# Loads of the first block, the order of the first loads, and matmuls on ones at the head of an attention and MLP kernel

## Chip and metric

The kernel runs on one NeuronCore of a Trainium2 chip. The metric is the device time of one execution in microseconds; lower is better. Before the change it was 308.45 us, the median of three runs (308.12 to 308.74).

## What is computed

Sliding-window attention with a linear bias (ALiBi), and behind it a two-layer MLP with a squared ReLU. Cut to what matters:

```python
# q, k, v: (8, 8, 576, 64) float32;  w_in: (512, 2048);  w_out: (2048, 512)
rel = pos[:, None] - pos[None, :]
bias = slopes[:, None, None] * (-abs(rel))
mask = (rel >= 0) & (rel < 128)
attn = softmax(where(mask, q @ k.T / 8 + bias, -1e9))
x = (attn @ v).transpose(0, 2, 1, 3).reshape(4608, 512)
out = square(maximum(x @ w_in, 0)) @ w_out          # (4608, 512) float32
```

## The kernel before

**Tiles.** Each of the 8 sequences of 576 tokens is cut into five blocks of 128, 128, 128, 128 and 64 tokens; a block holds all 8 heads, so its k, q and v are 128 x 512 each. There are 40 blocks, and 9 groups of 512 tokens for the MLP. Because the window is 128, a block of queries needs its own keys and those of the block before it.

**Work of a block** (`attention(m)`): k and q are turned on TensorE by eight transposes into one PSUM tile (`tp`, L331) and copied to `kqT` in two halves (L304 on VectorE, L306 on ScalarE). The scores are 8 or 16 matmuls (`ps_s`, L361), ScalarE takes the exponential (`P`, L374), VectorE multiplies by a mask that holds both bias and window (L382), TensorE multiplies with v (`pv`, L397, where a column of ones in `vt` gives the row sum), VectorE divides (L418, L423) into `x`, and four transposes (`xp`, L442) with a copy (L304) put the block into `xT`. From block 10 the first transposes, and from block 13 the last, are done by the DMA queue of SyncE (SP) instead.

**Work of a group**: 16 columns of `w_in` chunks give `h` (L477), ScalarE takes the ReLU (`rt`, L487), VectorE or ScalarE squares it (`g`, L495, L497), and `w_out` is applied: plainly in group 0 (L628), in the others by a Strassen-like scheme of seven products (L559) on sums of blocks. Groups 0 and 1 take `h` block by block (`SPLIT`), since their tokens arrive one block at a time.

**Loads.** All loads are issued by GpSimd (POOL), which casts fp32 to bf16 on the way: k, q, v of a block (L290, 128 KB each in bf16), `w_in` in four quarters of columns (L256) and `w_out` in four quarters of rows (L263), 512 KB each. `FIRST` (L162) gives the order of the first ones: `b0` is block 0, `i0` the first quarter of `w_in`, `o0` that of `w_out`. Eight loads can be under way: the ninth waits for the first to land. k and q have four buffers in a ring, v has six.

**Order.** Nothing is ordered by hand. Every piece of work is a `Task` with the engines that can do it, a duration, a key, and the tasks and buffers that it needs. `Plan.order()` (L57) plays the tasks through once, always taking the one that can start earliest, lowest key first, and each engine's queue then holds its tasks in the order of the planned starts. On the chip an engine works its queue in that order, and an instruction that waits holds up all behind it. The durations and delays are the plan's own; `COLD` (L42) is the planned time up to which a task of TensorE counts double (L113), and L115 to L117 say when a planned load lands:

```python
dur = t.engs[e] * (2 if e == "PE" and st < self.COLD else 1)
if t.dma is not None:
    at = max(st + dur + 900.0, self.dma_free)
    self.dma_free = at + t.dma
    t.end = self.dma_free + 900.0
```

**Head of the kernel.** GpSimd writes `dist` with an iota (L208); VectorE makes `ident`, which the transposes need, and `far` and `dist` out of it (L214, L220 to L223); ScalarE makes the eight `masks` (L234). VectorE also sets the ones in `vt` (L240, L242).

Of the kernel before, what the change touches and what calls it, by code (L numbers as in the profile page):

```python
# [8 lines left out]
FP32 = mybir.dt.float32  # L9
BF16 = mybir.dt.bfloat16  # L10
# [26 lines left out]
class Plan:  # L37
# [1 line left out]

    LAT = {"PE": 260.0, "ACT": 290.0, "DVE": 270.0, "POOL": 200.0, "SP": 2200.0}  # L40
    BEGIN = {"POOL": 1250.0}
    COLD = 15000.0  # L42

    def __init__(self, bufs):
        self.tasks = []
# [11 lines left out]
    def order(self):  # L57
        used = {tag: [] for tag in self.bufs}
        free = {}
        cand = {}  # L60
        left = {}
        for t in self.tasks:
            left[t] = len(t.deps)
            for d in t.deps:
                d.users.append(t)
            for e in t.engs:
                free.setdefault(e, self.BEGIN.get(e, 800.0))
                cand.setdefault(e, [])
        for t in self.tasks:
            if not left[t]:  # L70
                for e in t.engs:
                    cand[e].append(t)

        def avail(t):
            at = t.ready
            more = {}
            for s in t.acq:
                if s.idx is not None:
                    continue
                u = used[s.tag]  # L80
                n = self.bufs[s.tag]
                more[s.tag] = more.get(s.tag, 0) + 1
                i = len(u) + more[s.tag] - 1 - n
                if i >= 0:
                    old = u[i]
                    if old.left:
                        return None
                    at = max(at, old.freed)
            return at

        done = []
        n_all = len(self.tasks)
        while len(done) < n_all:
            best = None
            for e, c in cand.items():
                lo = None
                for t in c:
                    a = avail(t)
                    if a is None:
                        continue  # L100
                    st = max(a, free[e])
                    k = (st, t.key, t.seq)
                    if lo is None or k < lo[0]:
                        lo = (k, t)
                if lo is not None and (best is None or lo[0][0] < best[0]):
                    best = (lo[0][0], e, lo[1])
            if best is None:
                raise RuntimeError("plan is stuck: " + repr([
                    (e, t.key, [s.tag for s in t.acq if avail(t) is None]) for e, c in cand.items() for t in c
                    if e != "POOL"][:40]))  # L110
            st, e, t = best
            t.eng, t.start = e, st
            dur = t.engs[e] * (2 if e == "PE" and st < self.COLD else 1)  # L113
            if t.dma is not None:
                at = max(st + dur + 900.0, self.dma_free)  # L115
                self.dma_free = at + t.dma
                t.end = self.dma_free + 900.0  # L117
            else:
                t.end = st + dur + (self.LAT[e] if t.lat is None else t.lat)
            free[e] = st + dur  # L120
            for x in t.engs:
                cand[x].remove(t)
            for s in t.acq:
                if s.idx is not None:
                    continue
                s.idx = len(used[s.tag]) % self.bufs[s.tag]
                used[s.tag].append(s)
            for s in t.rel:
                s.left -= 1
                s.freed = max(s.freed, t.end)  # L130
            for u in t.users:
                left[u] -= 1
                u.ready = max(u.ready, st + dur if e == "PE" and "PE" in u.engs else t.end)
                if not left[u]:
                    for x in u.engs:
                        cand[x].append(u)
            done.append(t)
        done.sort(key=lambda t: (t.start, t.seq))
        return done
# [3 lines left out]
def kernel(  # L143
    ctx: ExitStack, tc: tile.TileContext, q, k, v, moe_w_in, moe_w_out, out
):
    nc = tc.nc

    B, H, S, D = q.shape
# [8 lines left out]
    C = d_model // 128  # L157
# [1 line left out]
    NG = NT // 512  # L159
    NBLK = B * NKB  # L160

    FIRST = "b0 i0 b1 i1 b2 i2 b3 i3 b4 b5 b6 o0 b7 o1 b8 o2 b9 o3"  # L162
    SPLIT = ([(0, 128), (128, 256), (256, 384), (384, 512)], [(0, 256), (256, 512)])

    KQ_DMA, X_DMA = 10, 13
# [2 lines left out]
    const = ctx.enter_context(tc.tile_pool(name="const", bufs=1))  # L168
    psum = ctx.enter_context(tc.tile_pool(name="psum", bufs=2, space=bass.MemoryType.PSUM))
    work = ctx.enter_context(tc.tile_pool(name="work", bufs=2))  # L170

    ident = const.tile([128, 128], BF16)
# [14 lines left out]
    kq = ring("kq", size["kq"], [128, 2, d_model])  # L187
# [14 lines left out]
    def mm(n):  # L202
        return max(n, 64) / 2.4 + 1.5
# [4 lines left out]
        nc.gpsimd.iota(dist, pattern=[[-128, 2], [1, 128]], base=128, channel_multiplier=-1,  # L208
                       allow_small_or_imprecise_dtypes=True)

    t_iota = plan.add({"POOL": 360.0}, -9e5 + 0.012, build_iota)

    def build_ident():
        nc.vector.tensor_single_scalar(ident, dist[:, 1], 0.0, op=ALU.is_equal)  # L214
# [8 lines left out]
        nc.vector.tensor_tensor(dist, dist, far, op=ALU.add)  # L223

    t_dist = plan.add({"DVE": 1300.0}, -9e5 + 0.5, build_dist, [t_ident])
    t_mask = []

    def place(h):
# [50 lines left out]
    def load_block(m, key):  # L279
        b, kb = divmod(m, NKB)  # L280
        n = blk[kb]
        s_in[m, "k"] = s_in[m, "q"] = Slot("kq")
        s_in[m, "v"] = Slot("v")
        for i, (nm, src) in enumerate((("k", k), ("q", q), ("v", v))):
            sl = s_in[m, nm]

            def emit(i=i, src=src, sl=sl, nm=nm):
                o = (vt[sl.idx][0:n, :, 0:D] if nm == "v"
                     else kq[sl.idx][0:n, i].rearrange("s (h d) -> s h d", h=H))
                nc.gpsimd.dma_start(o, src[b, :, kb * 128:kb * 128 + n, :].rearrange("h s d -> s h d"))  # L290
            t_in[m, nm] = load(key + 0.01 * i, 1050.0 * n / 128, emit, [t_ones] if nm == "v" else [], [sl])
# [10 lines left out]
    def copy(task, o, i):  # L302
        if task.eng == "DVE":
            nc.vector.tensor_copy(o, i)  # L304
        else:
            nc.scalar.activation(o, i, AF.Copy)  # L306

    def attention(m):
# [10 lines left out]
        if kq_by_dma:  # L319
            def turn_kq():  # L320
                nc.sync.dma_start_transpose(kqT[sk.idx], kq[s_in[m, "k"].idx].rearrange("s t f -> s (t f)"))
            t_kq = [plan.add({"SP": 2000.0}, due - 80, turn_kq, [t_in[m, "k"], t_in[m, "q"]], [sk],
                             [s_in[m, "k"]], dma=1400.0)]
        else:
            slot = Slot("h" if first else "a")
            last = None
            for i in range(2 * C):
                def emit(i=i):
                    if i == 0:
                        slot.tile = psum.tile([128, 1024], BF16, tag=slot.tag, bufs=plan.bufs[slot.tag], name="tp")  # L330
                    nc.tensor.transpose(slot.tile[:, i * 128:(i + 1) * 128],  # L331
                                        kq[s_in[m, "k"].idx][:, i // C, (i % C) * 128:(i % C + 1) * 128], ident)
                last = plan.add({"PE": mm(128)}, due - 56, emit,
                                [last, t_ident, t_in[m, "kq"[i // C]]] + ([t_in[m, "q"]] + chain["tp"] if i == 0 else []),
                                [slot, sk] if i == 0 else [], [s_in[m, "k"]] if i == 2 * C - 1 else [])
            chain["tp"] = [last]
            t_kq = []
            for i in range(2):
                def evac(i=i):
                    copy(t_kq[i], kqT[sk.idx][:, i * C:(i + 1) * C, 0:n],  # L340
                         slot.tile[:, i * 512:(i + 1) * 512].rearrange("p (c s) -> p c s", c=C)[:, :, 0:n])
                t_kq.append(plan.add(both if first else {("DVE", "ACT")[i]: both[("DVE", "ACT")[i]]},
                                     due - 56, evac, [last], [], [slot]))
        t_kq_of[m] = t_kq


# [41 lines left out]
        for hf in range(2):  # L388
            slot_v = Slot("o" if m < 5 else "h")
            last = None  # L390
            for hi in range(4):
                h = 4 * hf + hi
                for part, mk in parts:
                    def emit(h=h, hi=hi, part=part, mk=mk, slot_v=slot_v):
                        if hi == 0 and part == p0:
                            slot_v.tile = psum.tile([128, 512], FP32, tag=slot_v.tag, bufs=plan.bufs[slot_v.tag], name="pv")
                        nc.tensor.matmul(  # L397
                            slot_v.tile[:, hi * (D + 1):(hi + 1) * (D + 1)],
                            Pt[sP.idx][:, place(h), part, :], vt[s_in[mk, "v"].idx][:, h, :],
                            start=part == p0, stop=part == 1)  # L400
# [242 lines left out]
    key = 0  # L643
# [15 lines left out]

    done = plan.order()  # L660
    kernel.plan = done
    with tc.manual_schedule():
        for t in done:
            t.emit()


# [28 lines left out]
```

## Time and profile before

| | us |
|---|---|
| median of three runs | 308.45 |
| the profiled execution | 308.27 |
| its span, first to last instruction | 306.1 |
| TensorE busy | 289.8 |
| VectorE busy | 212.2 |
| ScalarE busy | 200.0 |
| GpSimd busy | 107.6 |

The profile is of one execution. Times in its rows are counted in us from the first instruction. Engines are named PE (TensorE), PEld (its weight loads), DVE (VectorE), ACT (ScalarE), POOL (GpSimd) and SP (SyncE). A row of the timeline has start, length, engine, line, operation, output and inputs, how many instructions are merged in it, and in brackets how long the engine had been idle and what ended that. A row of the loads has the size of one transfer and the us from its issue to its landing. A row of the waits has who waited for what, us in total, how often, and the longest.

### The profile page before, as it was taken

What the parts mean: (1) busy time and instruction counts of PE and PEld (TensorE: products, weight loads), DVE (VectorE), ACT (ScalarE), POOL (GpSimd) and SP (SyncE); (2) the same over time, 40 slices, a digit from 0 to 9 for tenths busy, and PEclk for the clock granted to TensorE, in tenths of its full rate; (3) what the DMA queues carried; (4) which work ended last, traced back from release to release, by engine and by line L of the source; (5) the groups of instructions that cost most, each with busy time, mean ns of one, the idle gap of its engine ahead of it and who ended that gap; (6) DMA issues with size and microseconds to landing.
All of it is one profiled execution on the core that took longest, in us unless ns stands there. A gap on an engine that the chain in (4) does not pass through costs nothing.

```text
span 306.1 us, 7855 instructions
## 1 busy us (share of the span) xinstructions
PE 289.8 (95%) x3076; PEld 205.9 (67%) x3076; DVE 212.2 (69%) x633; ACT 200.0 (65%) x395; POOL 107.6 (35%) x133
## 2 busy tenths in 40 slices
PE   1489999999999999999999999999999999999995
PEld 1279987686866677666666666666766676666783
DVE  4348888749968786678758776677677785545622
ACT  4178894759769666767767787777667785564410
POOL 8747938626265444226361327132200000000000
PEclk9999999999999999999999999999999999999999
DMA  8999999999999999999999999999884112201223
GB/s 60 179 175 166 151 189 173 130 184 139 151 151 144 164 157 169 155 154 182 165 153 166 156 139 149 130 165 146 139 55 120 30 42 62 69 0 36 69 72 103
DMA packets 170901, 39.31 MB, mean 128 GB/s; under 512 B 158064, under 2 KB 170352, under 8 KB 170864
## 3 DMA queue, kind: packets, MB, share of 16 engines
q0 software_dynamic: 116736, 18.36, 93.9%
q1 hardware_dynamic: 54128, 20.46, 41.3%
q8 instruction: 24, 0.39, 0.5%
q14 instruction: 13, 0.11, 0.1%
HBM read 36.70 MB, written 9.44 MB: 151 GB/s over the span
## 4 chain that ended last, share of the span: by engine, by line
PE 92%; DMA 3%; DVE 2%; POOL 2%; ACT 1%; issue 0%; POOLq 0%; DVEq 0%
PE h L477 42%; PE o L559 32%; PE ps_s L361 6%; PE pv L397 6%; PE o L628 4%; DMA kq<-in_q_dram 3%; PE tp L331 1%; POOL kq L290 1%; PE xp L442 1%; ACT kqT L306 1%; DVE w_mix L273 0%; DVE kqT L304 0%; POOL vt L290 0%; DVE osb L593 0%; POOL w_in_sb L256 0%
## 5 line engine op out<-in xcount | busy, mean ns | idle before, releaser
L477 PE MATMUL h<-xT,w_in_sb 128*128 128x512 bf16 (+2 forms) x832 | 150.8, 316 | 0.3 <-DVE x L423 0.3
L487 ACT ACTIVATE rt<-h 128x512 bf16<-128x512 f32 x144 | 86.0, 600 | 61.9 <-PE h L477 54.2
L477 PEld LDWEIGHTS <-w_in_sb 128*128 128x128 bf16 x832 | 71.0, 99 | 35.4 <-DVE x L423 0.8
L374 ACT ACTIVATE P<-ps_s 128x512 bf16<-128x512 f32 (+1 forms) x160 | 71.1, 520 | 9.7 <-PE ps_s L361 9.5
L495 DVE TENSOR_TENSOR g<-rt 128x512 bf16<-128x512 bf16 x91 | 38.3, 422 | 35.1 <-ACT rt L487 34.4
L382 DVE TENSOR_TENSOR P<-P,masks 128x512 bf16<-128x512 bf16 (+1 forms) x160 | 54.4, 364 | 8.0 <-ACT P L374 6.5
L559 PEld LDWEIGHTS <-g 128*128 128x128 bf16 x512 | 47.9, 98 | 15.1
L290 POOL DMA_DIRECT2D kq<-in_k_dram x40 | 34.2, 855 | 55.6 <-DMA kqT<-kq 48.4
L290 POOL DMA_DIRECT2D vt<-in_v_dram x40 | 34.1, 856 | 52.8 <-PE pv L397 46.6
L559 PEld LDWEIGHTS <-S 128*128 128x128 bf16 x384 | 35.8, 98 | 11.7 <-issue 0.7
L559 PE MATMUL o<-w_mix,S 128*128 128x256 bf16 x256 | 38.7, 273 | 0.0
L559 PE MATMUL o<-w_mix,g 128*128 128x256 bf16 x256 | 37.5, 273 | 0.0
L559 PE MATMUL o<-w_out_sb,g 128*128 128x256 bf16 x256 | 36.9, 273 | 0.0
L290 POOL DMA_DIRECT2D kq<-in_q_dram x40 | 34.3, 857 | 2.0 <-DMA kq<-in_k_dram 1.3
L497 ACT ACTIVATE g<-rt 128x512 bf16<-128x512 bf16 x53 | 33.5, 632 | 1.3
L423 DVE TENSOR_TENSOR x<-pv,rec 128x256 bf16<-128x256 f32 (+1 forms) x80 | 33.3, 417 | 1.1
L397 PEld LDWEIGHTS <-P 128*128 128x128 bf16 x576 | 27.3, 98 | 8.9 <-DVE P L382 1.2
L397 PE MATMUL pv<-vt,P 128*128 128x65 bf16 x576 | 31.5, 194 | 0.6 <-DVE P L382 0.6
L418 DVE RECIPROCAL rec<-pv 128x4 f32<-128x4 f32 (+1 forms) x80 | 14.2, 177 | 14.6 <-PE pv L397 14.2
L361 PEld LDWEIGHTS <-kqT 64*128 64x128 bf16 x576 | 15.7, 96 | 11.1 <-issue 8.9
L361 PE MATMUL ps_s<-kqT 64*128 64x128 bf16 (+1 forms) x320 | 20.1, 216 | 0.8 <-DVE kqT L304 0.8
L361 PE MATMUL ps_s<-kqT,kqT 64*128 64x128 bf16 (+1 forms) x256 | 17.0, 214 | 1.4 <-ACT kqT L306 1.4
(41 smaller groups left out, 190.6 us busy)
## 6 DMA issues: line engine op xcount, KB each, us to landing
out_dram<-osb SPq DMA_DIRECT2D x35, 256.0 KB, 4.3
kq<-in_k_dram POOLq DMA_DIRECT2D x32, 128.0 KB, 7.1
kq<-in_q_dram POOLq DMA_DIRECT2D x32, 128.0 KB, 7.4
vt<-in_v_dram POOLq DMA_DIRECT2D x32, 128.0 KB, 8.2
w_in_sb<-in_moe_w_in_dram POOLq DMA_DIRECT2D x4, 512.0 KB, 9.8
w_out_sb<-in_moe_w_out_dram POOLq DMA_DIRECT2D x4, 512.0 KB, 10.0
kq<-in_k_dram POOLq DMA_DIRECT2D x8, 64.0 KB, 9.2
kq<-in_q_dram POOLq DMA_DIRECT2D x8, 64.0 KB, 8.9
```

The source lines that it names most:

```text
L290: nc.gpsimd.dma_start(o, src[b, :, kb * 128:kb * 128 + n, :].rearrange("h s d -> s h d"))
L361: nc.tensor.matmul(slot_s[2 * (c // 2) + half].tile.rearrange("p (c t q) -> p c t q", c=2, t=2)[:, c % 2, part, 0:n], kqT[sk_of[mk].idx][r ...
L374: nc.scalar.activation(view(Pt[sP.idx][:, 2 * i:2 * i + 2]), view(slot_s[i].tile.rearrange("p (c t q) -> p c t q", c=2, t=2)), AF.Exp, bia ...
L382: nc.vector.tensor_tensor(pt, pt, view(masks[:, 2 * i:2 * i + 2]), op=ALU.mult)
L397: nc.tensor.matmul(slot_v.tile[:, hi * (D + 1):(hi + 1) * (D + 1)], Pt[sP.idx][:, place(h), part, :], vt[s_in[mk, "v"].idx][:, h, :], star ...
L418: nc.vector.reciprocal(srec.tile[0:n, :], pv[0:n, :, D])
L423: nc.vector.tensor_tensor(xt[sx.idx][0:n, hf * 256:(hf + 1) * 256].rearrange("p (h e) -> p h e", h=4), pv[0:n, :, 0:D], srec.tile[0:n, :]. ...
L477: nc.tensor.matmul(slot.tile[:, f * w:(f + 1) * w], w_in_sb[:, cc, (fc + f) * 128:(fc + f + 1) * 128], xT[:, cc, g * 512 + lo:g * 512 + hi ...
L487: nc.scalar.activation(srt.tile, slot.tile, AF.Relu, bias=0.0, scale=1.0)
L495: nc.vector.tensor_tensor(o, i, i, op=ALU.mult)
L497: nc.scalar.activation(o, i, AF.Square)
L559: nc.tensor.matmul(bank.tile[:, t * 256:(t + 1) * 256], left(g, what, j)[:, t * 128:(t + 1) * 128], right(by, j), start=opens and j == 0 a ...
```

## The change

- k and q of block 0 are loaded as fp32 into two buffers of the pool `osb`, by the queues of SP (k) and ACT (q), and cast to bf16 by two VectorE copies. v of block 0 stays with GpSimd.
- Among GpSimd's first loads block 1 stands ahead of the first quarter of `w_in`, block 2 ahead of the second, block 3 ahead of the third and fourth. The iota goes to the head of GpSimd's queue.
- k and q of a block are turned as two chains of four transposes, with the eviction of k as soon as its own four are planned to be done, still in one PSUM tile. Block 0's evictions are both VectorE's.
- VectorE writes a tile of ones. TensorE starts with seven matmuls of 512 columns on it, and as the program is put out, where TensorE's planned start of a task leaves a gap between 6 and 12.5 us of planned time, 128-column matmuls on ones are put in for about 70% of it. Their results are not used. In the built program these are 3, 2 and 16, ahead of block 0's transposes, block 0's scores and block 0's product with v.
- In the plan, the time up to which TensorE is slower becomes 9 us, and a task of 250 ns or more counts 1.4 times there; early loads start sooner, move 1.2 times longer and land later. So the order changes on all engines, throughout.

```diff
-    COLD = 15000.0
+    COLD = 9000.0
+    FILL = 12500.0
...
-            dur = t.engs[e] * (2 if e == "PE" and st < self.COLD else 1)
+            dur = t.engs[e] * (1 if e != "PE" or st > self.COLD else 2 if t.engs[e] < 250 else 1.4)
             if t.dma is not None:
-                at = max(st + dur + 900.0, self.dma_free)
-                self.dma_free = at + t.dma
-                t.end = self.dma_free + 900.0
+                early = st < self.COLD
+                at = max(st + dur + (700.0 if early else 900.0), self.dma_free)
+                self.dma_free = at + t.dma * (1.2 if early else 1.0)
+                t.end = self.dma_free + (1300.0 if early else 900.0)
...
-    FIRST = "b0 i0 b1 i1 b2 i2 b3 i3 b4 b5 b6 o0 b7 o1 b8 o2 b9 o3"
+    FIRST = "b0 b1 i0 b2 i1 b3 i2 i3 b4 b5 b6 o0 b7 o1 b8 o2 b9 o3"
...
-    t_iota = plan.add({"POOL": 360.0}, -9e5 + 0.012, build_iota)
+    t_iota = plan.add({"POOL": 360.0}, -9e5 - 1, build_iota)
...
+    ones_w = const.tile([128, 512], BF16)
+    slot_w = Slot("o")
+    scratch = {}
+
+    def build_warm():
+        nc.vector.memset(ones_w, 1.0)
+
+    def warm(n, w):
+        for _ in range(n):
+            nc.tensor.matmul(scratch["tile"][:, 512 - w:512], ones_w[:, 0:128], ones_w[:, 0:w], start=True, stop=True)
+
+    def first_warm():
+        scratch["tile"] = psum.tile([128, 512], FP32, tag="o", name="warm")
+        warm(7, 512)
+
+    t_warm = plan.add({"DVE": 300.0}, -9e5 - 2, build_warm)
+    plan.add({"PE": 2100.0}, -9e5, first_warm, [t_warm], [slot_w], [slot_w])
...
+            if m == 0 and nm != "v":
+                st = Slot("osb")
+
+                def raw(src=src, st=st, nm=nm):
+                    st.tile = work.tile([128, 512], FP32, tag="osb", bufs=plan.bufs["osb"], name="raw")
+                    (nc.sync if nm == "k" else nc.scalar).dma_start(
+                        st.tile.rearrange("s (h d) -> s h d", h=H), src[b, :, 0:n, :].rearrange("h s d -> s h d"))
+
+                def cast(i=i, st=st, sl=sl):
+                    nc.vector.tensor_copy(kq[sl.idx][:, i], st.tile)
+                t_raw = plan.add({"SP" if nm == "k" else "ACT": 450.0}, -2e6, raw, [], [st], dma=1050.0)
+                t_in[m, nm] = plan.add({"DVE": 470.0}, key + 0.01 * i, cast, [t_raw], [sl], [st])
+                continue
...
-            for i in range(2 * C):
...
+            for j, nm in enumerate("kq"):
+                last = None
+                for i in range(C):
...
+                        nc.tensor.transpose(slot.tile[:, (j * C + i) * 128:(j * C + i + 1) * 128],
+                                            kq[s_in[m, nm].idx][:, j, i * 128:(i + 1) * 128], ident)
...
+                chain["tp"] = [last]
+
+                def evac(j=j):
+                    copy(t_kq[j], kqT[sk.idx][:, j * C:(j + 1) * C, 0:n],
+                         slot.tile[:, j * 512:(j + 1) * 512].rearrange("p (c s) -> p c s", c=C)[:, :, 0:n])
+                t_kq.append(plan.add({"DVE": both["DVE"]} if m == 0 else both if first else
+                                     {("DVE", "ACT")[j]: both[("DVE", "ACT")[j]]}, due - 56, evac, [last], [], [slot]))
...
+    idle = 6000.0
     with tc.manual_schedule():
         for t in done:
+            if t.eng == "PE":
+                if idle < t.start < plan.FILL:
+                    warm(int(0.7 * (t.start - idle) / (107.0 if t.start < plan.COLD else 56.0)), 128)
+                idle = max(idle, t.start + t.engs["PE"] * (2 if t.start < plan.COLD else 1))
             t.emit()
```

More of the change, by code (lines that the diff above doesn't have):

```diff
@@ L325, in attention @@
             slot = Slot("h" if first else "a")
-            last = None
-            for i in range(2 * C):
[L328 to L335, printed above, removed]
@@ L336, in attention @@
-            chain["tp"] = [last]
-            t_kq = []
[L338 to L343, printed above, removed]
+            t_kq = []
@@ new lines, in attention, with emit @@
+            for j, nm in enumerate("kq"):
+                last = None
+                for i in range(C):
+                    def emit(i=i, j=j, nm=nm):
+                        if i == 0 and j == 0:
+                            slot.tile = psum.tile([128, 1024], BF16, tag=slot.tag, bufs=plan.bufs[slot.tag], name="tp")
+                        nc.tensor.transpose(slot.tile[:, (j * C + i) * 128:(j * C + i + 1) * 128],
+                                            kq[s_in[m, nm].idx][:, j, i * 128:(i + 1) * 128], ident)
+                    last = plan.add({"PE": mm(128)}, due - 56, emit,
+                                    [last, t_ident, t_in[m, nm]] + (chain["tp"] if i == 0 else []),
+                                    [slot, sk] if i == 0 and j == 0 else [], [s_in[m, nm]] if j == 1 and i == C - 1 else [])
+                chain["tp"] = [last]
[4 more added lines that the diff above has]
+                                     {("DVE", "ACT")[j]: both[("DVE", "ACT")[j]]}, due - 56, evac, [last], [], [slot]))
@@ L396, in emit @@
                             slot_v.tile = psum.tile([128, 512], FP32, tag=slot_v.tag, bufs=plan.bufs[slot_v.tag], name="pv")
+                            if slot_v.tag == "o":
+                                scratch["tile"] = slot_v.tile
                         nc.tensor.matmul(
```

## The prediction

> **What bounds the kernel now.** I read the page's head and chain first, then TensorE's waits, then TensorE's timeline to 31 us, then the loads' issues and landings.
>
> ```profile
> span 306.1 us, 7855 instructions
> PE 289.8 (95%) x3076; PEld 205.9 (67%) x3076; DVE 212.2 (69%) x633; ACT 200.0 (65%) x395; POOL 107.6 (35%) x133
> PEclk9999999999999999999999999999999999999999
> PE 92%; DMA 3%; DVE 2%; POOL 2%; ACT 1%; issue 0%; POOLq 0%; DVEq 0%
> ```
>
> TensorE is busy 289.8 of 306.1 us and is 92% of the chain that ends last. What is not TensorE lies at the start, as its waits say (total, times, longest):
>
> ```profile
> PE tp L331 <- DMA kq<-in_k_dram: 8.3, 2, 5.1
> PE ps_s L361 <- ACT kqT L306: 1.4, 2, 0.7
> PE o L559 <- DVE osb L593: 0.5, 1, 0.5
> PE h L477 <- DVE x L423: 0.3, 1, 0.3
> ```
>
> The two waits for k are blocks 0 and 1. The timeline (start, length, what, idle before) gives the places:
>
> ```profile
> 7.80 0.61 PE L361 MATMUL ps_s<-kqT 64*128 64x128 bf16 x8 [0.85 <-DVE kqT L304]
> 8.97 1.18 PE L397 MATMUL pv<-vt,P 128*128 128x65 bf16 x8 [0.56 <-DVE P L382]
> 13.38 0.61 PE L331 MATMUL tp<-ident,kq 128*128 128x128 bf16 x4 [3.23 <-DMA kq<-in_k_dram]
> 16.93 3.24 PE L477 MATMUL h<-xT,w_in_sb 128*128 128x128 bf16 x32
> 20.22 0.61 PE L331 MATMUL tp<-ident,kq 128*128 128x128 bf16 x8
> 20.67 0.59 PE L397 MATMUL pv<-vt,P 128*128 128x65 bf16 x9
> 21.98 0.23 PE L361 MATMUL ps_s<-kqT,kqT 64*128 64x128 bf16 x2 [0.71 <-ACT kqT L306]
> 22.76 1.28 PE L477 MATMUL h<-xT,w_in_sb 128*128 128x128 bf16 x20
> 30.32 0.61 PE L331 MATMUL tp<-ident,kq 128*128 128x128 bf16 x8
> ```
>
> So h begins at 16.93, and from about 20 us on TensorE hardly stops. The same h costs 3.24/32 = 0.101 us at first and 1.28/20 = 0.064 later with its tail (about 0.056 apart, from the eight transposes at 20.22: 0.61 less one of some 0.22 over seven). The PEclk row shows no step there, yet the pace nearly doubles: up to about 20 us TensorE runs at half pace. Time can be won only ahead of 22 us, and stays won only if nothing later waits. The loads (POOL's issue, then one load's size and us to landing):
>
> ```profile
> 1.25 1.02 POOL L290 DMA_DIRECT2D kq<-in_k_dram  x1 [0.80 <-POOLq L679]
> 2.26 0.89 POOL L290 DMA_DIRECT2D kq<-in_q_dram  x1
> 4.55 0.76 POOL L256 DMA_DIRECT2D w_in_sb<-in_moe_w_in_dram  x1
> 5.29 0.91 POOL L290 DMA_DIRECT2D kq<-in_k_dram  x1
> 7.89 0.80 POOL L256 DMA_DIRECT2D w_in_sb<-in_moe_w_in_dram  x1
> 17.86 0.75 POOL L256 DMA_DIRECT2D w_in_sb<-in_moe_w_in_dram  x1 [1.29 <-DMA w_in_sb<-in_moe_w_in_dram]
> 19.79 0.68 POOL L290 DMA_DIRECT2D kq<-in_q_dram  x1
> ```
>
> ```profile
> kq<-in_k_dram POOLq DMA_DIRECT2D x1, 128.0 KB, 3.8
> kq<-in_q_dram POOLq DMA_DIRECT2D x1, 128.0 KB, 4.0
> w_in_sb<-in_moe_w_in_dram POOLq DMA_DIRECT2D x1, 512.0 KB, 7.9
> kq<-in_k_dram POOLq DMA_DIRECT2D x1, 128.0 KB, 8.0
> w_in_sb<-in_moe_w_in_dram POOLq DMA_DIRECT2D x1, 512.0 KB, 9.7
> w_in_sb<-in_moe_w_in_dram POOLq DMA_DIRECT2D x1, 512.0 KB, 10.0
> kq<-in_q_dram POOLq DMA_DIRECT2D x1, 64.0 KB, 9.3
> ...
> GB/s 0 0 0 96 90 90 109 123 182 189 160 158 180 203 201 162 158 176 205 201 165 157 173 211 198 167 157 155 161 147 118 103 114 179 158 182 157 163 181 203
> ```
>
> Row by row, issue plus landing: k0 5.05, q0 6.26, first quarter of w_in (w0) 12.45, k1 13.29, w1 17.59, w3 27.86, q4 29.09. The last row is the DMA rate in slices of 1 us. Two paces follow. Settled: k1 comes 0.84 after w0, so a block's three loads take 2.5; from k1 to w1 there are q1, v1 and w1, so a w_in quarter takes 4.3 - 1.7 = 2.6 (check: w1 to w3 is two blocks and two quarters, 10.2; the rows say 10.27). Early: q0 comes 1.21 after k0, at 90 to 109 GB/s against 157 to 211 later.
>
> **The loads.** The change issues k0 and q0 as fp32 from SP and ACT at about 0.75 (their queues are empty there; ACT's table load and masks wait for nothing that this issue delays), and POOL's queue becomes iota, k1, q1, v0, v1, w0, block 2, w1, block 3, w2, w3. No row shows an fp32 load of 256-byte pieces on these queues. The nearest are the last stores:
>
> ```profile
> out_dram<-osb SPq DMA_DIRECT2D x3, 256.0 KB, 2.2
> out_dram<-osb SPq DMA_DIRECT2D x2, 128.0 KB, 1.7
> ```
>
> By bytes, 256 KB lands 2.2 after issue, at 3.0. By pieces, the second 128 rows cost 0.5, and 1024 pieces would take 1.7 + 7 x 0.5 = 5.2, landing at 6.0. I take 4.5, the middle; POOL's own k0 took 3.8 with its 1.02 of issue. Five more 128 KB loads (the other raw one, k1, q1, v0, v1) at the early pace: 4.5 + 5 x 1.21 = 10.55. Then w0: 2.6 at the settled pace, or 5.0 as before (12.45 - 6.26 less one 1.21 for v0). It now moves when the rate row is already at 160 and more: 3.3, so w0 lands at 13.9. Ends: 3.0 + 5 x 0.84 + 2.6 = 9.8, and 6.0 + 6.05 + 5.0 = 17.0. Each later load follows at the settled pace: w1 at 13.9 + 2.5 + 2.6 = 19.0 (1.4 later than before, since block 2 goes ahead of it), q3 20.7, w3 26.7, q4 27.9 (q4 was 1.23 behind w3).
>
> [...]
>
> **Head of the kernel.** The casts are two DVE copies of 128x512. The nearest rows:
>
> ```profile
> 7.00 0.76 DVE L304 COPY kqT<-tp 128x512 bf16<-128x512 bf16 x2 [1.68 <-PE tp L331]
> 21.33 0.60 ACT L306 ACTIVATE kqT<-tp 128x512 bf16<-128x512 bf16 x1 [0.52 <-DVE kqT L304]
> 8.62 1.12 DVE L382 TENSOR_TENSOR P<-P,masks 128x256 bf16<-128x256 bf16 x4 [0.87 <-ACT P L374]
> ```
>
> 0.38 to 0.42 each, up to 0.6 for fp32; DVE idled 1.68 there, which covers them. On DVE the four kqT copies of blocks 0 and 1 now stand ahead of block 0's mask products, so these wait for q1 (4.5 + 3 x 1.21 = 8.1): block 0's pv begins near 9.8 instead of 8.97. That costs nothing, since block 1's ps_s, which waited until 15.97, can follow at about 10.5, and its exponentials and most of its pv lie in the wait for w0. If that cover went, the price would be the 0.8 of that delay.
>
> **Matmuls on ones.** Seven of 512 columns at half pace are 4 x 0.101 x 7 = 2.8 us, three of 128 another 0.3: from about 1.4 to 4.6, ahead of the first cast. Two and sixteen more stand ahead of block 0's ps_s and pv: 1.8 us at half pace, 1.0 at full, while DVE copies and multiplies. Cost nothing; without that cover 1.8, still ahead of w0. What they buy is the pace. The half pace cost 32 x (0.101 - 0.056) = 1.4 us before; now h is cut by waits until 22 us, so I book the pace within the next count and not again.
>
> [...]
>
> **Count at 22.8 us.** Before, 32 h are done there, and block 2's pv, block 3's transposes and ps_s are not. After, from 13.9 on, TensorE does 16 h each of blocks 0 and 1 on w0, all of attention 2 but pv's end, then at 19.0 twelve h on w1, block 3's transposes at 20.7, eleven h, block 3's ps_s near 22: 55 h. Ahead: 23 x 0.056 = 1.3, pv 0.5 (nine take 0.59 at 20.67; its last few are still to come), xp 4 x 0.056, transposes 8 x 0.056, ps_s 0.45 (eight took 0.61 at half pace, sixteen are needed): 2.9 us. The loads cap it: q4 at 27.9 is 1.2 earlier, and before, TensorE took q4 1.2 after it landed (30.32 against 29.09), so at most 2.4 is kept.
>
> **Split transposes.** In blocks 0 to 9 k's four transposes are now evicted ahead of q's four. Both share one PSUM tile, and in the built program q's transposes wait for the eviction of k in blocks 0 to 5, 8 and 9; before, none did. Behind such a transpose everything on TensorE queues. One costs the eviction (0.42 on DVE, 0.60 on ACT) less what stands between: in blocks 2 and 3 it hides behind q's landing, 0.84 after k's; in 4, 5, 8, 9 five h or a few transposes (0.28) stand there, leaving 0.1 to 0.3. Ends: nothing, or the 0.71 that ps_s waited for the same copies at 21.98. I take 0.7 in all. The rest of the order is replanned; I book nothing, as the waits after 22 us were single and 1.5 in total.
>
> Sum: 2.4 - 0.7 = 1.7 us. The profiled execution took 308.27 (span 306.1 and 2.2 around it), 0.2 under the median 308.45: 308.3 - 1.7 = 306.6.
>
> **Rivals.**
> 1. The engines run at the settled pace from the start, w0 near 11. For: three queues feed them at once. Against: 90 GB/s early. Then block 1's exponentials bind, h starts near 12.5, 1.4 earlier still; the cap moves by the 2.9 of w0 and no longer binds: 2.9 + 1.4 - 0.7 = 3.6 us, 304.7.
> 2. The loads are not earlier: the fp32 pieces take from the same engines what they save, w3 stays at 27.9. Only the 1.2 of slack at q4 is left, less 0.7: 307.8.
> 3. Slower: the split transposes. Place: TensorE's queue, six splits (blocks 2 to 5, 8, 9). Price: 0.7 each, 4.2, if the evictions stand behind ACT's exponentials; against a lead of 2.4: +1.8, 310.1. It decides from 0.4 a split. For: the 0.71 row. Against: h stands in between, and DVE does three of them.
> 4. The ones do not open the clock: the 3.2 us of work between 13.9 and 19.0 become 6.4 in 5.1: 1.3 less, 307.9.
>
> **How the numbers follow.** Forecast 0.45 (305.5 to 307.8), rival 1 0.15, rival 2 0.13, rival 3 0.17, rival 4 0.10. No change is within 0.2% of 308.45, 307.8 to 309.1, about what a measurement can tell. Faster: 0.45 + 0.15 and a half of rivals 2 and 4, near 0.70; same 0.12; slower 0.18. Range: 304.2 to 309.2 leaves out most of rival 3 and little below.
>
> **What would show it.** Right: raw loads landing at 4 to 5, k1 before w0, the first h at 13 to 15 and spaced 0.056, no wait over 0.5 at the q transposes. Wrong: h at 16 or later, h still at 0.1 after 15 us, waits of TensorE for kqT's copies adding to over 2 us after 22 us, or waits for k and w_in beyond 25 us.

## The result, and the profile after

The changed kernel takes 307.00 us, the median of 20 runs (304.84 to 308.27), against 307.78 (20 runs, 306.79 to 308.95) of the kernel before. The ratio is 0.9962, with a 95% interval of 0.9948 to 0.9977: 0.7 to 1.6 us faster. The quotient of the two medians is 0.9975, near the upper end of this interval. Run once more beside later experiments it came out at 0.9951 (0.9934 to 0.9968). The profiled execution took 307.52 us, above its median, so its own gain over the profile before is only 0.5 us of span; the shape below is the same in the profile of the second round (first h at 14.52, and the same waits of 0.9 and 0.2 us on copies of kqT behind 22 us).

The head of the page, of the changed kernel:

```profile
span 305.6 us, 7920 instructions
PE 294.4 (96%) x3104; PEld 207.7 (68%) x3104; DVE 216.3 (71%) x639; ACT 198.6 (65%) x392; POOL 105.9 (35%) x131
PE 93%; DVE 2%; ACT 2%; DMA 1%; issue 0%; DVEq 0%
```

In the chain that ends last, the DMA went from 3% to 1%, and DVE and ACT hold 2% each now. The timeline of TensorE, changed kernel (start, length, what, idle before and its releaser):

```profile
1.46 3.48 PE L237 MATMUL warm<-ones_w 128*128 128x512 bf16 x10 [1.46 <-DVE vt L259]
6.41 0.93 PE L365 MATMUL tp<-ident,kq 128*128 128x128 bf16 x7 [1.46 <-DVE kq L314]
7.85 0.69 PE L365 MATMUL tp<-ident,kq 128*128 128x128 bf16 x5 [0.52 <-DVE kqT L336]
8.69 0.61 PE L394 MATMUL ps_s<-kqT 64*128 64x128 bf16 x8
9.63 1.91 PE L237 MATMUL warm<-ones_w 128*128 128x128 bf16 x16
11.34 0.43 PE L432 MATMUL pv<-vt,P 128*128 128x65 bf16 x4
14.67 0.89 PE L512 MATMUL h<-xT,w_in_sb 128*128 128x128 bf16 x13
23.09 0.23 PE L394 MATMUL ps_s<-kqT,kqT 64*128 64x128 bf16 x2
28.11 0.39 PE L365 MATMUL tp<-ident,kq 128*128 128x128 bf16 x4
28.97 0.38 PE L365 MATMUL tp<-ident,kq 128*128 128x128 bf16 x4 [0.19 <-ACT kqT L338]
32.49 0.22 PE L365 MATMUL tp<-ident,kq 128*128 128x128 bf16 x1 [0.51 <-DVE kqT L336]
```

The first h stands at 14.67 instead of 16.93, and thirteen of it take 0.89 us: 0.056 apart, full pace. The sixteen ones at 9.63 still take 1.91, or 0.107 each, so the pace steps up between 11 and 14 us instead of near 20. Block 3's scores are reached at 23.09. The fifth block's transposes come at 28.11 instead of 30.32, 2.2 us ahead. Then the two waits on the eviction of k appear, and the lead over the kernel before begins to go. The loads, changed kernel (POOL's issues, the sizes and us to landing of the raw loads, of the first and second quarter of w_in and of the fifth block's q, and the rate in slices of 1 us):

```profile
4.98 0.79 POOL L275 DMA_DIRECT2D w_in_sb<-in_moe_w_in_dram  x1
8.55 0.78 POOL L275 DMA_DIRECT2D w_in_sb<-in_moe_w_in_dram  x1
16.09 0.68 POOL L322 DMA_DIRECT2D kq<-in_q_dram  x1 [0.27 <-PE h L512]
```

```profile
raw<-in_q_dram ACTq DMA_DIRECT2D x1, 256.0 KB, 4.5
raw<-in_k_dram SPq DMA_DIRECT2D x1, 256.0 KB, 3.8
w_in_sb<-in_moe_w_in_dram POOLq DMA_DIRECT2D x1, 512.0 KB, 7.9
w_in_sb<-in_moe_w_in_dram POOLq DMA_DIRECT2D x1, 512.0 KB, 9.4
kq<-in_q_dram POOLq DMA_DIRECT2D x1, 64.0 KB, 10.5
...
GB/s 0 16 176 276 167 152 152 148 181 189 170 156 165 195 207 176 160 161 206 199 202 208 204 166 155 155 167 136 133 127 90 151 194 169 162 175 176 204 204 209
```

The raw loads land 3.8 and 4.5 after their issue, w0 at 4.98 + 7.9 = 12.9, w1 at 8.55 + 9.4 = 18.0, q4 at 16.09 + 10.5 = 26.6. Before, slices 4 to 7 moved 90, 90, 109 and 123 GB/s; now 167, 152, 152 and 148. So w0 lands 0.45 us later than before, with three more small loads ahead of it (six instead of three), and q4 is 2.5 us earlier.

TensorE's busy time by stretches, kernel before and then the changed kernel (stretch, its length, busy us, instructions, granted clock, and the loads' busy share and GB/s):

```profile
28.00:34.00 6.00, 6.00 (x125) 1.00 1.87 137
34.00:46.00 12.00, 12.00 (x217) 1.00 1.71 180
```

```profile
28.00:34.00 6.00, 5.29 (x105) 1.00 1.58 144
34.00:46.00 12.00, 11.51 (x196) 1.00 1.64 189
```

In the 18 us from 28 to 46 the changed TensorE idles 1.2 us where the old one had no idle time. The scores that start at 43.45 in the profile before start at 42.92 here, so of the 2.2 us 0.5 are left, and the idle time is 1.2 of the 1.7 that went. Its waits behind 22 us in the changed kernel, as far as they are on copies of kqT, are

```profile
PE tp L365 <- DVE kqT L336: 0.9, 2, 0.5
PE tp L365 <- ACT kqT L338: 0.2, 1, 0.2
```

### The profile page after: what moved, and what is told of

The parts are those of the page before. It is cut to its first block, busy times and chain, and to the rows that moved or that the text cites. A ratio compares the mean times of both kernels' runs of the same rounds, so it can differ in the third digit from the quotient of the medians.

```text
span 305.6 us, 7920 instructions
## 1 busy us (share of the span) xinstructions
PE 294.4 (96%) x3104; PEld 207.7 (68%) x3104; DVE 216.3 (71%) x639; ACT 198.6 (65%) x392; POOL 105.9 (35%) x131
## 3 DMA queue, kind: packets, MB, share of 16 engines
q10 hardware_dynamic: 1040, 0.26, 0.4%
## 4 chain that ended last, share of the span: by engine, by line
PE 93%; DVE 2%; ACT 2%; DMA 1%; issue 0%; DVEq 0%
PE h L512 41%; PE o L594 32%; PE ps_s L394 6%; PE pv L432 6%; PE o L663 4%; PE tp L365 2%; DMA raw<-in_q_dram 1%; PE xp L477 1%; ACT P L407 1%; DVE kqT L336 1%; PE warm L237 1%; ACT rt L522 1%; DVE kq L314 0%; DVE P L415 0%; ACT kqT L338 0%
## 5 line engine op out<-in xcount | busy, mean ns | idle before, releaser
L512 PEld LDWEIGHTS <-w_in_sb 128*128 128x128 bf16 x832 | 70.1, 98 | 36.1 <-issue 1.0
L530 DVE TENSOR_TENSOR g<-rt 128x512 bf16<-128x512 bf16 x89 | 37.6, 422 | 38.7 <-ACT rt L522 37.6
L594 PE MATMUL o<-w_mix,g 128*128 128x256 bf16 x256 | 38.2, 273 | 0.0
L594 PE MATMUL o<-w_mix,S 128*128 128x256 bf16 x256 | 37.9, 273 | 0.0
L532 ACT ACTIVATE g<-rt 128x512 bf16<-128x512 bf16 x55 | 34.8, 633 | 1.3
L322 POOL DMA_DIRECT2D kq<-in_q_dram x39 | 33.5, 858 | 4.3 <-DMA kq<-in_q_dram 1.7
L594 PE MATMUL o<-w_out_sb,S 128*128 128x256 bf16 x128 | 17.9, 273 | 0.5 <-DVE osb L628 0.5
```

What stands on the lines that cost most here:

```text
L512: nc.tensor.matmul(slot.tile[:, f * w:(f + 1) * w], w_in_sb[:, cc, (fc + f) * 128:(fc + f + 1) * 128], xT[:, cc, g * 512 + lo:g * 512 + hi ...
L530: nc.vector.tensor_tensor(o, i, i, op=ALU.mult)
L532: nc.scalar.activation(o, i, AF.Square)
L594: nc.tensor.matmul(bank.tile[:, t * 256:(t + 1) * 256], left(g, what, j)[:, t * 128:(t + 1) * 128], right(by, j), start=opens and j == 0 a ...
```

## The experiments

All twelve compute the whole result. Ratios are to the kernel before, run on the same chip, with 95% intervals.

**The split of the transposes (e1).** The changed kernel, with k's eviction put out only behind q's last transpose:

```diff
+            held[t_kq[0]] = last
...
+            if t in held and held[t] not in emitted:
+                waiting.setdefault(held[t], []).append(t)
+                continue
             t.emit()
+            for u in waiting.pop(t, []):
+                u.emit()
```

TensorE's and VectorE's queues hold the same instructions in the same order; on ScalarE one eviction swaps places with a ReLU. Only what waits for what differs, the wait of 0.52 in block 0 (at 7.85) included.

> The changed kernel, in which the eviction of k is put out only after q's last transpose, so that q's transposes no longer wait for it; TensorE's and VectorE's queues hold the same instructions in the same order. Theory (the split eats the lead): the waits of q's transposes on kqT, 0.2 at 28.97, 0.5 at 32.49 and 0.4 later, go, the lead over the kernel before stays above 1 us at 45 us instead of 0.34, and the time is 0.7 to 1.1 us below the changed kernel's: ratio to before 0.992 to 0.994. Rival (the loads cap the lead whatever the queue does): the waits turn up at other instructions and the ratio stays at 0.996.

Measured: 305.38 us, ratio 0.9927 (0.9903 to 0.9951). TensorE's waits behind 22 us, e1:

```profile
PE ps_s L395 <- DVE kqT L336: 0.7, 1, 0.7
PE o L596 <- DVE osb L630: 0.5, 1, 0.5
PE o L665 <- ACT rt L524: 0.2, 1, 0.2
```

No transpose waits for a copy any more. The one wait for kqT that is left stands ahead of scores, as in the kernel before. The scores that start at 43.45 before and at 42.92 in the changed kernel start at 41.35. The theory holds: the waits of the split cost 0.9957 - 0.9927 = 0.3%, 0.9 us, with the mean of the changed kernel's two ratios. The intervals overlap, so the size is rough; but only four of the changed kernel's 32 runs are below 305.67, the slowest of e1's six.

**The split taken out of the plan as well (e7).** The transposes and evictions of the kernel before, the rest of the text as changed. The plan orders anew, and 31 matmuls on ones fall into the waits instead of 21:

```diff
-            for j, nm in enumerate("kq"):
-                last = None
-                for i in range(C):
+            last = None
+            for i in range(2 * C):
...
+                last = plan.add({"PE": mm(128)}, due - 56, emit,
+                                [last, t_ident, t_in[m, "kq"[i // C]]] + ([t_in[m, "q"]] + chain["tp"] if i == 0 else []),
+                                [slot, sk] if i == 0 else [], [s_in[m, "k"]] if i == 2 * C - 1 else [])
+            chain["tp"] = [last]
+            t_kq = []
+            for i in range(2):
```

> The changed kernel with the eight transposes of a block in one chain and both evictions behind it, as before; the plan orders anew. Theory (the split is the whole of the difference between the changed kernel and e1): ratio 0.992 to 0.994, lead over before above 1.2 us at 45 us. Rival (the new order costs the lead as well, e1 was lucky in keeping the old queues): 0.995 to 0.998.

Measured: 305.13 us, 0.9934 (0.9909 to 0.9959); the changed kernel beside it 306.14. The profiled execution has a span of 302.8. Its transposes of blocks 4 to 6, in the timeline of e7:

```profile
27.42 0.61 PE L363 MATMUL tp<-ident,kq 128*128 128x128 bf16 x8
30.15 0.61 PE L363 MATMUL tp<-ident,kq 128*128 128x128 bf16 x8
33.53 0.61 PE L363 MATMUL tp<-ident,kq 128*128 128x128 bf16 x8
```

Before they stood at 30.32, 33.03 and 36.69: a lead of 2.9, 2.9 and 3.2 us that stays, and the span is 3.3 shorter (the medians, 305.13 against 307.58, differ by 2.4). As expected, and the same time as e1 by another route, though here the order and the number of ones differ too.

**The matmuls on ones (e2, e5, e6, e10).** e2 is the changed kernel without them, and e5 is e1 without them:

```diff
     def warm(n, w):
-        for _ in range(n):
-            nc.tensor.matmul(scratch["tile"][:, 512 - w:512], ones_w[:, 0:128], ones_w[:, 0:w], start=True, stop=True)
+        pass
...
     def first_warm():
-        scratch["tile"] = psum.tile([128, 512], FP32, tag="o", name="warm")
-        warm(7, 512)
+        pass
```

e6 is e1 with the head's seven alone, e10 is e1 with the 21 in the waits alone:

```diff
-                if idle < t.start < plan.FILL:
+                if False:
```

```diff
-        warm(7, 512)
+        warm(0, 512)
```

> The changed kernel without its 28 matmuls on ones, all else in the same order (VectorE still writes the tile). Theory (the ones buy the pace): TensorE still takes 0.1 us a matmul at the first h and for some 4 us behind it, and the time is 0.5 to 1.0 us above the changed kernel's: ratio 0.998 or more. Rival (the sixteen ahead of pv hold it up by 0.6 and the pace would have come anyway): pv of block 0 at 10.8 instead of 11.34, first h near 14.1 instead of 14.67, ratio 0.994 to 0.996.

> Late eviction of k as in e1, and no matmuls on ones. Theory (the ones open the clock by 12 us instead of 16 and that is worth time): 0.5 to 1.1 us above e1, ratio 0.995 to 0.997. Rival (the half pace falls into waits): first h 0.5 to 0.9 earlier since the sixteen no longer hold up pv, time within 0.3 us of e1, ratio 0.992 to 0.993.

> Late eviction as in e1, with the seven matmuls on ones at the head alone, without the 2 and 16 in the waits. Theory (the sixteen hold up pv by 0.6 and open nothing that the head's do not): first h by 12.8 instead of 13.33, ratio 0.991 to 0.992. Rival (the sixteen keep TensorE in work up to the step of the clock near 11 to 12 us): the step comes near 15 us as without ones, ratio 0.994 to 0.997, as e5.

> Late eviction as in e1, the 3, 2 and 16 matmuls on ones in the waits, without the seven of 512 columns at the head. Theory (only the ones just ahead of the scores and pv open the clock, the head's are forgotten in the wait of 1.3 us behind them): step of the clock near 11 to 13 us as in e1, ratio 0.992 to 0.994. Rival (both are needed): the step comes at 15 us or later, ratio 0.996 to 0.999 as with the head's alone.

Measured: e2 0.9997 (0.9976 to 1.0019), against 0.9951 and 0.9962 with them. e5 0.9991 (0.9972 to 1.0009), e6 0.9983 (0.9965 to 1.0000), e10 0.9922 (0.9896 to 0.9948), against e1's 0.9927. The first thirteen h in the timelines of e5, e6 and e10:

```profile
13.80 1.57 PE L512 MATMUL h<-xT,w_in_sb 128*128 128x128 bf16 x13
```

```profile
13.78 1.57 PE L514 MATMUL h<-xT,w_in_sb 128*128 128x128 bf16 x13
```

```profile
14.01 0.89 PE L514 MATMUL h<-xT,w_in_sb 128*128 128x128 bf16 x13
```

Without ones, or with the head's alone, h starts as early and runs at half pace (0.11 us apart); with those in the waits it runs at full pace (0.056 apart). The ones are worth 0.6% or 2 us in the kernel with late eviction (e5 against e1), 0.4% in the changed one (e2), and all of it comes from the 21 in the waits; the seven at the head bring nothing that these runs can tell. e5 and e6 came out above both of their forecasts, which ended at 0.997. The rival named for e2 was right that pv and h come sooner without the sixteen (pv at 10.16, first h at 13.74) and wrong that this would pay. In e5 h did not even come sooner: 13.80 against 13.33 in e1's profile.

**The raw loads (e3, e9).** e3 is the changed kernel with k and q of block 0 loaded by GpSimd:

```diff
-            if m == 0 and nm != "v":
+            if False:
```

e9 is the kernel before with the raw loads and the casts alone:

```diff
             sl = s_in[m, nm]
+            if m == 0 and nm != "v":
+                st = Slot("osb")
...
+                t_raw = plan.add({"SP" if nm == "k" else "ACT": 450.0}, -2e6, raw, [], [st], dma=1050.0)
+                t_in[m, nm] = plan.add({"DVE": 470.0}, key + 0.01 * i, cast, [t_raw], [sl], [st])
+                continue
```

> The changed kernel with k and q of block 0 loaded and cast by GpSimd again, ahead of block 1; the plan orders anew. Theory (the raw loads win the time): k1 and q1 land 1.8 later and all behind them with them, first h at 16 or later, ratio 0.999 to 1.003. Rival (the chain through VectorE binds the head, not the loads): without the casts the transposes start as early, first h at 14.5 to 15.5, ratio 0.996.

> The kernel before with k and q of block 0 by the queues of SP and ACT and the two casts, nothing else changed; the plan orders anew and puts the first quarter of w_in at the head of GpSimd's queue. Theory (the raw loads bring the time, since all other loads move up by two): w1 and w3 land 1.5 to 2.5 earlier than before, ratio 0.993 to 0.997. Rival (they need the ones and the order of blocks to be worth anything): first h still at half pace to 19 us, ratio 0.998 to 1.001.

Measured: e3 308.61 us, 1.0042 (1.0022 to 1.0062), slower than the kernel before; e9 307.49 us, 0.9978 (0.9957 to 0.9999). w0 among the loads of e3, and its first h in the timeline:

```profile
w_in_sb<-in_moe_w_in_dram POOLq DMA_DIRECT2D x1, 512.0 KB, 8.0
```

```profile
14.71 1.89 PE L512 MATMUL h<-xT,w_in_sb 128*128 128x128 bf16 x16 [0.40 <-DMA w_in_sb<-in_moe_w_in_dram]
```

Issued at 6.69, w0 lands at 14.7, 1.8 later than in the changed kernel, as expected, and h now waits for it. That it would start at 16 was wrong, and the ratio is above both forecasts. It also runs at half pace (1.89 for 16), so e3's loss is not the loads' alone: without the raw loads the planned waits, and with them the ones, fall elsewhere. e9 lies between its two forecasts, and its first h, at 14.35, runs near half pace (1.73 for 17). So the raw loads, with the order that the plan makes of them, bring 0.2%, and how much of the 0.8% between e3 and the changed kernel is theirs stays open.

**The order of the first loads (e4).**

```diff
-    FIRST = "b0 b1 i0 b2 i1 b3 i2 i3 b4 b5 b6 o0 b7 o1 b8 o2 b9 o3"
+    FIRST = "b0 i0 b1 i1 b2 i2 b3 i3 b4 b5 b6 o0 b7 o1 b8 o2 b9 o3"
```

> The changed kernel with the old order of the first loads, w_in's quarters each behind one block; the plan orders anew. Theory (blocks first wins the time): w0 lands near 9 to 10 but k1 only near 11, attention of block 1 comes 4 us later, and the lead at 23 us is 1 us or less: ratio 0.999 or more. Rival (the order of bytes is nothing to TensorE, their sum is): h starts earlier, the lead at 23 us is the same 2 us, ratio 0.995 to 0.997.

Measured: 307.05 us, 0.9977 (0.9958 to 0.9996). w0 lands near 9.4, as expected, and h starts no sooner (14.56). The interval touches both forecasts. Set against the changed kernel's 0.9957 it speaks for 0.2% in favour of the new order, less than the intervals can tell; and the plan puts 32 ones into the waits here instead of 21. So this part is not settled.

**The plan's delays (e8, e11).** e7 with the old delays and slow time:

```diff
-    COLD = 9000.0
+    COLD = 15000.0
...
-            dur = t.engs[e] * (1 if e != "PE" or st > self.COLD else 2 if t.engs[e] < 250 else 1.4)
+            dur = t.engs[e] * (2 if e == "PE" and st < self.COLD else 1)
...
-                early = st < self.COLD
+                early = False
```

> The unsplit kernel of e7 with the plan's old delays and slow time (15 us at double, loads landing 900 ns after their pace); the plan orders anew, and 13 matmuls on ones stand in the waits instead of 31. Theory (the new delays make the planned order fit what happens): waits of TensorE for loads or copies of 1 us and more come back between 14 and 30 us, ratio 0.996 to 0.999. Rival (the order is as good with either): 0.993 to 0.995, as e7.

> The kernel of e8 once more, to see whether it stands clear of e7 (unsplit, new delays, 0.9934). Theory (the old delays give an order at least as good): ratio 0.986 to 0.992. Rival (its four runs were a lucky few): 0.992 to 0.995, as e7.

Measured: e8 304.60 us, 0.9882 (0.9849 to 0.9916); the same kernel again 305.10 us, 0.9918 (0.9886 to 0.9950). TensorE's waits for loads did come back, in e8:

```profile
PE tp L363 <- DMA kq<-in_k_dram: 1.4, 1, 1.4
PE tp L363 <- DMA kq<-in_q_dram: 0.8, 2, 0.5
```

Two of the three stand in the head (at 13.76 and 14.61), the third, of 0.5, behind 22 us. The new delays bring no gain that shows; whether the old ones are better is not settled, as e7's interval meets both. This kernel and e7 beat the kernel before. Against the changed one (0.9934 to 0.9968, 0.9948 to 0.9977) only e8's first interval stands clear.

e8 also shows how far the account of the head reaches. Its first h starts at 15.46, later than in the changed kernel, and seven h at 16.12 take 0.94 us, half pace (0.12 apart). Yet no kernel here is faster. What its order does better is open.

**The changed kernel again (c1).**

> The changed kernel itself once more, as the measure for the three runs beside it: ratio to before 0.995 to 0.998.

Measured: 306.14 us, 0.9951 (0.9934 to 0.9968).

## Why the prediction was right, step by step

The forecast was 1.7 us faster, 306.6; measured are 0.7 to 1.6 us in the first comparison and 1.0 to 2.0 in the second. The best values, 1.2 and 1.5, are somewhat below the forecast. Direction and size hold. Of the mechanism the loads, the cost of the split and the worth of the pace are shown; what sets the first h was wrong.

- *The raw loads land at 4.5*: 4.5 for k, 5.2 for q, which is 0.2 beyond the 4 to 5 that was named. Right in the main, but k's early landing brings nothing. VectorE's casts in the changed kernel:

```profile
5.22 1.12 DVE L314 CAST kq<-raw 128x512 bf16<-128x512 f32 x2 [0.51 <-DMA raw<-in_q_dram]
```

The first cast starts when q lands, and k's transposes, TensorE's first, wait until both casts are done (6.41). The plan lets k's load land after q's, so it puts q's cast ahead of k's. The working did not look at their order, and no run here has it the other way.
- *w0 at 13.9, behind five small loads at the early pace*: 12.9. The slow early pace that the profile before showed was not there any more: slices 4 to 7 move 148 to 167 GB/s instead of 90 to 123. The step was wrong in the good direction by 1.0, and q4 by 1.3 (26.6 against 27.9).
- *First h when w0 lands, 13.9*: 14.67, 1.8 after w0. It was not the loads that set it but the head's chain: two casts, transposes that wait 0.52 for an eviction, and the sixteen ones that TensorE finishes ahead of pv (11.34 against the 9.8 of the working). With late evictions h stands at 14.01 (e10) and, where the first transposes also ran at full pace, at 13.33 (e1). So this step failed: w0 came 1.0 early and h 1.8 behind it, and that h still fell into the 13 to 15 that was named is luck.
- *55 h and block 3's scores by 22.8*: reached at 23.09.
- *At most 2.4 kept at the fifth block, by the loads*: 2.2 in place, but not for the reason given. q4 was there 1.5 us ahead of its transposes.
- *The splits cost 0.7*: 1.1 us of waits behind 22 us and 0.52 in block 0, and 0.9 us of time (e1). Right in kind, a little small; two of the waits, 0.52 and 0.51, pass the 0.5 that was named. As a rival they were priced at 4.2; they stayed far from it.
- *The ones cost nothing and may not open the clock*: with them the first h runs at full pace (0.056 apart, 0.11 in e2), and that is worth 0.4%, some 1.2 us, where the fourth rival had priced their failure at 1.3. They were not free: in the second profile of the changed kernel pv begins 0.9 later than in e2 (11.06 against 10.16) and the first h 0.8 (14.52 against 13.74), with the first transposes at the same time (6.13 and 6.07). That work on ones would bring the full pace was the author's expectation; the profile before has some 4.2 us of unbroken work (15.97 to 20.2) ahead of its step, and no row of it shows more. The working made no difference between the ones at the head and those in the waits; e6 (0.9983) and e10 (0.9922) show that only those in the waits matter.
- *The replanned order costs nothing*: not shown. In e7 the lead of about 3 us stays to the end. In the changed kernel 2.2 fall to 0.5 of span, of which the waits for copies are 1.1. What took the rest, some 0.6, is not settled.

Of the rivals, the second (loads no earlier) fell with q4 at 26.6. The first was half right about the pace of the loads (w0 at 12.9, between its 11 and the forecast's 13.9) and wrong that h would follow.

## What to carry to other kernels

In a kernel whose one engine is full, time won at the head counts only if that engine's queue has no new wait behind it (here 2.2 us of lead at the fifth block became 0.5): follow a lead at a few named instructions to the end. Before splitting a step to let a part of it go on sooner, look whether both parts share a tile; the second half may then wait for the reader of the first, as q's transposes did here for the eviction of k (0.52 us in block 0, 0.51 at 32.49). Idle matmuls paid here where they stood just ahead of the work that needed the pace, not at the head of the queue (0.9922 in e10 against 0.9983 in e6). And where an order comes from planned delays, see in the trace whether the first task of a chain waits behind one that nothing needs yet, as k's cast does here.

## What was not expected of the hardware

In e1 the pace of TensorE stepped back. Twelve transposes ran at full pace (0.84 us), and the sixteen ones 2 us later at half (1.91); in e10, without the head's ones, the same transposes ran at half (1.46; timeline of e1, then of e10):

```profile
6.07 0.84 PE L365 MATMUL tp<-ident,kq 128*128 128x128 bf16 x12 [1.33 <-DVE kq L314]
8.28 1.91 PE L237 MATMUL warm<-ones_w 128*128 128x128 bf16 x16
```

```profile
6.07 1.46 PE L365 MATMUL tp<-ident,kq 128*128 128x128 bf16 x12 [4.11 <-DVE kq L314]
```

So in e1 the full pace is there at 6 us and gone again at 8.3. A wait of 1.33 us stands ahead of those transposes and one of 0.51 between them and the sixteen ones. The granted clock shows something of it: 0.92 on average over the first 22 us of e1, where the kernel before and both profiles of the changed kernel have 1.00. It does not show the slow time ahead of the first step: it is 1.00 from 16 to 20 us in the kernel before, where h runs 0.101 apart, and 1.00 from 8 to 12 us in the changed kernel, where the sixteen ones take the same 1.91. In the changed kernel's two profiles, with the same instructions up to there, the transposes behind the head's ones ran at half pace (seven in 0.93, at 6.41 and at 6.13), and so did those of e6 behind the seven ones alone (twelve in 1.46). What decides between the two, no run here shows.

The other surprise is the loads' early rate. The rate in slices of 1 us in e3, where GpSimd alone issues and the small loads go first as in the changed kernel:

```profile
GB/s 0 0 0 92 94 116 146 136 143 116 130 170 152 157 154 184 206 190 169 161 183 196 205 206 206 180 163 174 139 141 117 129 129 160 192 189 160 150 152 181
```

Slices 4 and 5 move 94 and 116 GB/s, 90 and 90 in the kernel before; with the two raw loads beside them 167 and 152. The trace, split by queue, tells more than the sum. In the changed kernel a packet of a raw load counts 256 bytes (1040 of them, 0.26 MB, to a load) and one of a casting load of k or q 128 (1206 from 5 to 6 us, 0.15 MB), and in slice 5 no raw packet moves any more. Up to 6 us GpSimd's queue has moved 2079 packets there, 0.26 MB; e3's row gives 92, 94 and 116 KB for it, 0.30 MB, so its own loads are no further on. The raw loads' 2080 packets come on top, 1776 of them (0.45 MB) in slices 2 and 3, in which e3 moves 0.09 MB. So what is won is the early start of the raw loads, and two loads less for GpSimd's queue. Why this queue moves 94 and 116 KB in slices 4 and 5 of e3, and 856 and 1206 packets (0.11 and 0.15 MB) in the changed kernel, no run here tells.
